# Half of the query transposes in the preceding unit, and the last output chunk in two column halves, in a pooled-attention and mixer kernel

## The chip, the cores and the metric

The kernel runs on one core of one Trainium2 chip. The metric is the device time of one execution in microseconds (us). Before the change the median of five runs is 298.71 us (297.93 to 300.1).

## What is computed

Attention over pooled keys and values, for 8 batches of 8 heads, 576 positions and head dimension 64, followed by a token MLP and a channel MLP. Inputs and output are float32.

```
pool = 8                                       # 576 keys become 72
k_p = k.reshape(B, H, 72, 8, D).mean(axis=3)
v_p = v.reshape(B, H, 72, 8, D).mean(axis=3)
attn = softmax(q @ k_p.T / sqrt(D))
x = (attn @ v_p) as (B, S, H * D)              # 576 x 512 per batch
xt = x.transpose(0, 2, 1)
h = np.maximum(xt @ w_tok1, 0) @ w_tok2        # 576 -> 256 -> 576
u = x + h.transpose(0, 2, 1)
out = u + np.maximum(u @ w_ch1, 0) @ w_ch2     # 512 -> 1536 -> 512
```

## The kernel before

**Tiling.** The 576 positions of a batch are written as (p r), with 64 values of p and 9 of r. Four chunks of 128 rows take r = 0 to 7, two values of r each; the ninth is a tail of 64 rows. Two batches share a tail tile, so the four tail tiles make up one more channel-MLP job of 512 rows.

**Units.** The program is a head, which prepares batch 0, and nine units. Unit n (function `unit`) runs the channel MLP of batch n: twelve groups of four matmuls (L412), each followed by a relu into GT on ScalarE, or on VectorE for every fourth group (L417, L419); then four output chunks of twelve matmuls (L424), each followed by an addition of u on VectorE (L429) and two output transfers on SyncE's queue (L432). Unit 8 does this for the tails. `unit_steps` is a generator that yields after every second matmul, 48 times in a unit. Steps 0 to 23 belong to the first product, six steps to each output chunk after that.

**Side work.** Between those steps the attention and token MLP of batch n+1 are put in by a table written out by hand: FIRST for unit 0, LATER for all others. A table gives, for a step number, the names of pieces of work. The order in which these are issued is the order in every engine's queue; the engines wait for each other by semaphores. The pieces that matter here:

- Q0, Q1 (`qD`, L253): transposes of the q block, from batch 2 on. VectorE turns 32x32 blocks of qb into qD. Each piece has four stream transposes and serves two of the four pairs of heads.
- kpT (L209, L211): eight small transposes of the pooled keys on TensorE, then the copy kD on VectorE.
- e0, o0 to e3, o3 (`score`, L271, L277): two score matmuls each, and the exponential on ScalarE. They read kD and qD.
- av0 to av4 (L293, L305, L311): attention product, reciprocal and scaling.
- at0, at1 (L339, L330, L332): first token product with relu, on ScalarE for at0 and VectorE for at1.
- u0 to u4 (L354, L355): second token product and the addition of x. t0 to t4 (L364, L365): the transpose of u on TensorE, and its copy into uT, which the next unit's L412 reads. u4 and t4 make the shared tail and are done for odd batches only.

**Buffers and loads.** `unit(n)` first issues the loads of batch n+2 (`load`) on GpSimd's queue: keys, the q block qb (L110) and values, then `prepare` for batch n+1: a few VectorE memsets and the pooling of keys and values on GpSimd. qb and qD have two buffers each (in the pools `raw` and `att`), so the load of qb for batch n+2 waits until the transposes of batch n are done. In PSUM `ps_one` has three buffers, `ps_two` two, and `ps_tr`, which kpT and t0 to t4 share, one.

Of the kernel before, what the change touches and what calls it, by code (L numbers as in the profile page):

```python
# [8 lines left out]
FP32 = mybir.dt.float32  # L9
BF16 = mybir.dt.bfloat16  # L10
AF = mybir.ActivationFunctionType
ALU = mybir.AluOpType
# [7 lines left out]
def kernel(  # L20
# [14 lines left out]
    nc = tc.nc  # L35
    B, H, S, D = q.shape
    P = 128
    POOL = 8
    SP = S // POOL
    BP, BR = 64, S // 64  # L40
# [4 lines left out]
    HP = H // 2  # L45
    DM = H * D
    DT = moe_w_tok1.shape[1]
    DC = moe_w_ch1.shape[1]
    NM = DC // P
# [4 lines left out]
    att = ctx.enter_context(tc.tile_pool(name="att", bufs=2))  # L54
    mix = ctx.enter_context(tc.tile_pool(name="mix", bufs=2))
    gtp = ctx.enter_context(tc.tile_pool(name="gtp", bufs=1))
    outp = ctx.enter_context(tc.tile_pool(name="outp", bufs=4))
    ps_one = ctx.enter_context(tc.tile_pool(name="ps_one", bufs=3, space=bass.MemoryType.PSUM))
# [8 lines left out]
    w_ch2 = singles.tile([P, NM, DM], BF16)  # L67
# [8 lines left out]
    loaded = {}  # L76
# [57 lines left out]
    def load_ch1():  # L134
        for g in range(3):
            cols = slice(g * 512, (g + 1) * 512)
            nc.gpsimd.dma_start(out=w_ch1[:, :, cols], in_=moe_w_ch1[:, cols].rearrange("(c p) n -> p c n", p=P))

    def load_ch2():
        for g in range(3):  # L140
            nc.gpsimd.dma_start(out=w_ch2[:, 4 * g:4 * g + 4, :],
                                in_=moe_w_ch2[g * 512:(g + 1) * 512, :].rearrange("(c p) n -> p c n", p=P))
# [19 lines left out]
    def batch_steps(b):  # L162

        par, first, by_pe = b % 2, b == 0, b < BY_PE
        st = {}
# [1 line left out]
        lower = slice(par * BP, (par + 1) * BP)  # L167

        def prepare():
            kr, vr, qb = loaded.pop(b)  # L170
            kp = att.tile([SP, H, 2, D], BF16, name="kp") if by_pe else kps[par]
            vp = att.tile([SP, H, D + 1], BF16, name="vp")
            ex = att.tile([SP, H * S + BP], BF16, name="ex")
            nc.vector.memset(vp[:, :, D], float(POOL))
            nc.vector.memset(ex[:, H * S:], 0.0)
            st.update(kp=kp, vp=vp, qb=qb, ex=ex, kr=kr, vr=vr)
            if b > 1:
                for s in ("K0", "K1", "V0", "V1"):
                    name[s]()
            if by_pe:  # L180
                st["qT"] = att.tile([P, HP, 2, EV], BF16, name="qT")
            else:
                st["qD"] = att.tile([P, HP, S], BF16, name="qD")
                st["kD"] = att.tile([P, H * SP], BF16, name="kD")
            st["AT"] = att.tile([P, 2, DM], BF16, name="AT")
            st["x"] = mix.tile([P, 4, DM], BF16, name="x")
            st["u"] = mix.tile([P, 4, DM], BF16, name="u")
            st["uT"] = mix.tile([P, 4, 4 * P], BF16, name="uT")
            if par == 0:
                tails[b // 2] = mix.tile([P, DM], BF16, name="xt")  # L190
                nc.vector.memset(tails[b // 2], 0.0)
            st["xt"] = tails[b // 2]
# [11 lines left out]
        def kpT(h0, h1):  # L204
            def go():
                ps = ps_tr.tile([P, H, SP], BF16, name="pt")
                for h in range(h0, h1):
                    row = st["kp"][:, h].rearrange("j e d -> j (e d)" if by_pe else "j e l d -> j (e l d)")
                    nc.tensor.transpose(out=ps[:, h, :], in_=row, identity=ident[0:SP, 0:SP])  # L209
                if not by_pe:  # L210
                    nc.vector.tensor_copy(out=st["kD"], in_=ps.rearrange("p h j -> p (h j)"))  # L211
                    return
                for half in range(2):
                    rows = slice(half * D, (half + 1) * D)
                    copy = nc.scalar.copy if first and half == 0 else nc.vector.tensor_copy
                    copy(out=kT[rows, half, h0 * SP:h1 * SP], in_=ps[rows, h0:h1, :].rearrange("p h j -> p (h j)"))
            return go
# [28 lines left out]
                    nc.scalar.copy(out=dst, in_=ps)  # L246
            return go

        def qD(g):
            def go():  # L250
                for ph in range(2):
                    for db in range(2):
                        nc.vector.transpose(  # L253
                            out=st["qD"][db * 64:(db + 1) * 64, 2 * g:2 * g + 2, :].rearrange(
                                "m a (r j u) -> m a r j u", u=2, r=BR)[:, :, :, :, ph],
                            in_=st["qb"][ph * 64:(ph + 1) * 64, 2 * g:2 * g + 2, 0:BR * D].rearrange(
                                "m a (r d) -> m a r d", d=D)[:, :, :, db * 32:(db + 1) * 32])
            return go

        def score(hp, odd):  # L260
# [126 lines left out]
        name = {f"kpT{g}": kpT(g * HP, (g + 1) * HP) for g in range(2)}  # L387
# [3 lines left out]
            name[f"K{g}"], name[f"V{g}"] = pool("kr", g), pool("vr", g)  # L391
        for hp in range(HP):
            name[f"q{hp}"], name[f"o{hp}"], name[f"e{hp}"] = qT(hp), score(hp, 1), score(hp, 0)
        name["Q0"], name["Q1"] = qD(0), qD(1)
        for c in range(5):
            name[f"av{c}"], name[f"u{c}"], name[f"t{c}"] = av(c), u(c), uT(c)
            name[f"at_{c}"] = at_tile(c)
# [6 lines left out]
    def unit_steps(n, st):  # L404

        GT = gtp.tile([P, NM, 4 * P], BF16, name="GT")
        uT = uT_tails if n == B else st["uT"]
        u_all = u_tails if n == B else st["u"]
        for m in range(NM):
            ps = ps_one.tile([P, 512], FP32, name="p1")  # L410
            for kk in range(4):
                nc.tensor.matmul(out=ps, lhsT=w_ch1[:, kk, m * P:(m + 1) * P], rhs=uT[:, kk, :],  # L412
                                 start=(kk == 0), stop=(kk == 3))
                if kk == 1:
                    yield
            if m % 4 != 3 or n == 0:
                nc.scalar.activation(out=GT[:, m, :], in_=ps, func=AF.Relu)  # L417
            else:
                nc.vector.tensor_scalar(out=GT[:, m, :], in0=ps, scalar1=0.0, scalar2=None, op0=ALU.max)  # L419
            yield  # L420
        for c in range(4):
            ps = ps_one.tile([P, 512], FP32, name="p1")
            for m in range(NM):
                nc.tensor.matmul(out=ps, lhsT=GT[:, m, c * P:(c + 1) * P], rhs=w_ch2[:, m, :],  # L424
                                 start=(m == 0), stop=(m == NM - 1))
                if m % 2 == 1 and m < NM - 1:
                    yield
            o_sb = outp.tile([P, DM], FP32, name="o")
            nc.vector.tensor_tensor(out=o_sb, in0=ps, in1=u_all[:, c, :], op=ALU.add)  # L429
            for half in range(2):  # L430
                b, r = (2 * c + half, 8) if n == B else (n, 2 * c + half)
                nc.sync.dma_start(out=out[b].rearrange("(p r) n -> p r n", r=BR)[:, r, :],  # L432
                                  in_=o_sb[half * BP:(half + 1) * BP, :])
            yield
# [5 lines left out]
             16: "kpT1 V0", 17: "o1", 18: "e1", 19: "q2", 20: "o2 V1", 21: "e2", 22: "q3", 23: "o3", 24: "e3",  # L440
             25: "av0", 26: "av1", 27: "av2", 28: "av3", 29: "av4", 31: "at0", 32: "at1", 34: "U0", 35: "U1",
             36: "t0 U2", 38: "t1 U3", 39: "U4", 40: "t2", 42: "t3", 46: "t4"}
    LATER = {0: "Q0", 1: "kpT", 6: "Q1", 8: "e0", 10: "o0", 12: "e1", 13: "o1", 15: "e2", 17: "o2",
             18: "e3", 20: "o3", 23: "av0", 25: "av1", 27: "av2", 29: "av3", 31: "av4", 33: "at0", 34: "at1",
             37: "u0", 38: "u1", 39: "t0", 40: "u2", 41: "t1", 42: "u3", 43: "u4 t2", 45: "t3", 47: "t4"}
    warm = singles.tile([P, 512], BF16)

    def head(s):
# [13 lines left out]
    def unit(n, at):  # L462
        side = {}
        if n + 1 < B:
            load(n + 2)
            batches[n + 1][0]()
            side = batches[n + 1][1]
        for i, _ in enumerate(unit_steps(n, batches[n][2] if n < B else None)):
            for s in at.get(i, "").split() if side else []:
                if (n + 1) % 2 or s not in ("u4", "t4"):  # L470
                    (batches[0][1][s] if n == 0 and s[0] == "u" else side[s.lower() if s[0] == "U" else s])()

    with tc.manual_schedule(engines={PE, POOLE, DVE, ACT}):
        batches = [batch_steps(b) for b in range(B)]
        nc.vector.memset(warm, 0.0)
        load(0)
        nc.vector.memset(kTs[0][D:P, 0, :], 0.0)
        nc.vector.memset(kTs[0][0:D, 1, :], 0.0)
        nc.vector.memset(w_tok1[:, 4:6, :], 0.0)
        nc.vector.memset(w_tok2t, 0.0)  # L480
        load_tok()
        load_ch1()
        permute_tok2()
        load(1)
        load_ch2()
        batches[0][0]()
        for s in HEAD.split():
            head(s)
        nc.vector.memset(kTs[1][D:P, 0, :], 0.0)
        nc.vector.memset(kTs[1][0:D, 1, :], 0.0)  # L490
        for kp in kps:
            nc.vector.memset(kp, 0.0)
        unit(0, FIRST)
        for n in range(1, B + 1):
            unit(n, LATER)


# [28 lines left out]
```

The softmax here doesn't subtract the row's maximum and nothing guards it: scores larger than these inputs give would overflow.

## Time and profile before

| | |
|---|---|
| median of five runs | 298.71 us |
| the profiled execution | 298.45 us |
| its span, first to last instruction | 296.6 us |
| TensorE busy in the span | 280.7 us |
| VectorE, ScalarE, GpSimd busy | 178.1, 97.6, 133.8 us |
| units 1 to 6, each | 29.85 to 30.7 us |
| units 7 and 8, without side work | 20.7 us and, with the end, 25.5 us |
| granted TensorE clock | 1.0 throughout |

Busy TensorE time is the sum of its recorded matmuls, whose ends are modelled, so a short loss of pace inside it doesn't show as idle. Units 2, 4 and 6 begin at 98.6, 159.4 and 220.3 us of the span, units 3 and 5 at 129.3 and 190.1 us; units 3 and 5 follow on a unit that also holds u4 and t4. Times of single instructions are given in us from the start of the span.

### The profile page before, as it was taken

To read this page: it belongs to the slowest core of one execution; us is meant where nothing else is said; L and a number is where in the kernel's file an instruction comes from. 1 tells how busy PE (TensorE), PEld (TensorE's weight loads), DVE (VectorE), ACT (ScalarE), POOL (GpSimd) and SP (SyncE) were. 2 spreads that over 40 slices of the span, in tenths; PEclk is the share of its full clock that TensorE was granted. 3 is DMA by queue.
4 is the path that set the end of the run, shared out by engine and by line. 5 is a ranking of instruction groups with operands and counts; after the bars stand their busy time and mean duration, and the time that the engine had idled before them with its cause. 6 is when DMAs were issued, how large, how long until landed. Compare 5 with 4: busy or idle time off the path is not lost.

```text
span 296.6 us, 4482 instructions
## 1 busy us (share of the span) xinstructions
PE 280.7 (95%) x1796; PEld 145.2 (49%) x1796; DVE 178.1 (60%) x332; ACT 97.6 (33%) x176; POOL 133.8 (45%) x136
## 2 busy tenths in 40 slices
PE   8789888999999999999999999999999999999993
PEld 3464354454555455445544554445455545444441
DVE  4237956678477847786758675785578556121221
ACT  2353467003900390028102810173017300502400
POOL 8285115991699069904992599993000000000000
PEclk9999999999999999999999999999999999999999
DMA  7999999947661856183827481300320021114023
GB/s 139 208 204 204 205 200 189 169 104 138 98 113 41 147 87 110 43 144 44 140 50 125 72 140 46 71 2 0 70 69 5 2 63 46 35 35 106 0 56 88
DMA packets 26868, 28.25 MB, mean 95 GB/s; under 512 B 4960, under 2 KB 21728, under 8 KB 26848
## 3 DMA queue, kind: packets, MB, share of 16 engines
q0 software_dynamic: 20512, 17.35, 40.0%
q1 hardware_dynamic: 6048, 10.03, 13.9%
q10 hardware_dynamic: 288, 0.59, 0.7%
q8 instruction: 14, 0.23, 0.3%
q14 instruction: 6, 0.05, 0.0%
HBM read 35.85 MB, written 9.44 MB: 153 GB/s over the span
## 4 chain that ended last, share of the span: by engine, by line
PE 79%; DVE 12%; ACT 4%; DMA 3%; issue 2%; POOLq 0%
PE p L424 30%; PE p L412 23%; PE p L354 6%; DVE qD L253 6%; PE p L271 5%; PE p L339 5%; PE p L293 3%; DMA kr<-in_k_dram 3%; PE pt L364 2%; DVE o L429 2%; ACT ex L277 2%; ACT GT L417 1%; DVE x L311 1%; PE pt L452 1%; DVE kD L211 1%
## 5 line engine op out<-in xcount | busy, mean ns | idle before, releaser
L424 PE MATMUL p<-w_ch,GT 128*128 128x512 bf16 x432 | 111.0, 379 | 0.0
L412 PE MATMUL p<-uT,w_ch 128*128 128x512 bf16 x384 | 95.7, 379 | 1.6 <-ACT GT L417 1.6
L417 ACT ACTIVATE GT<-p 128x512 bf16<-128x512 f32 x84 | 49.9, 594 | 106.0 <-PE p L412 93.9
L412 PEld LDWEIGHTS <-w_ch 128*128 128x128 bf16 x432 | 41.5, 98 | 38.9 <-issue 2.5
L424 PEld LDWEIGHTS <-GT 128*128 128x128 bf16 x432 | 38.7, 98 | 36.6 <-issue 0.7
L277 ACT ACTIVATE ex<-p 72x576 bf16<-72x576 f32 (+1 forms) x64 | 40.3, 645 | 14.9 <-PE p L271 13.9
L419 DVE TENSOR_SCALAR GT<-p 128x512 bf16<-128x512 f32 x24 | 16.6, 692 | 40.4 <-PE p L412 40.2
L253 DVE STREAM_TRANSPOSE qD<-qb 64x576 bf16<-64x576 bf16 x48 | 39.1, 814 | 0.7
L110 POOL DMA_DIRECT2D qb<-in_q_dram x12 | 7.6, 634 | 52.8 <-DVE qD L253 38.0
L149 POOL TENSOR_TENSOR t<-t 72x512 f32<-72x512 f32 x24 | 30.3, 1264 | 1.9
L429 DVE TENSOR_TENSOR o<-p,u 128x512 f32<-128x512 f32 x32 | 22.0, 688 | 10.3 <-PE p L424 10.2
L355 DVE TENSOR_TENSOR u<-p,x 128x512 bf16<-128x512 f32 x32 | 21.9, 688 | 6.8 <-PE p L354 6.8
L148 POOL TENSOR_TENSOR t<-kr 72x1024 f32<-72x1024 bf16 x12 | 25.5, 2126 | 0.1
L148 POOL TENSOR_TENSOR t<-vr 72x1024 f32<-72x1024 bf16 x12 | 25.4, 2118 | 0.0
L271 PE MATMUL p<-qD,kD 128*72 128x288 bf16 x96 | 19.8, 288 | 2.9 <-DVE kD L211 2.9
L311 DVE TENSOR_TENSOR x<-p,den 128x512 bf16<-128x512 f32 x30 | 20.8, 692 | 1.0
L330 ACT ACTIVATE AT<-p 128x512 bf16<-128x512 f32 x8 | 4.8, 597 | 49.7 <-PE p L339 47.0
L293 PEld LDWEIGHTS <-ex 72*128 72x128 bf16 x320 | 15.2, 98 | 10.6 <-DVE x L311 2.2
L354 PE MATMUL p<-AT,w_tok 128*128 128x512 bf16 x64 | 19.0, 379 | 0.3 <-ACT GT L417 0.3
L271 PEld LDWEIGHTS <-kD 128*72 128x72 bf16 x96 | 10.4, 113 | 15.1 <-DVE kD L211 5.8
L293 PE MATMUL p<-vp,ex 72*128 72x65 bf16 x320 | 16.9, 194 | 0.5 <-DVE x L311 0.3
L332 DVE TENSOR_SCALAR AT<-p 128x512 bf16<-128x512 f32 x8 | 5.5, 692 | 17.3 <-PE p L339 16.4
(90 smaller groups left out, 243.5 us busy)
## 6 DMA issues: line engine op xcount, KB each, us to landing
out_dram<-o SPq DMA_DIRECT2D x72, 128.0 KB, 2.4
kr<-in_k_dram POOLq DMA_DIRECT2D x7, 576.0 KB, 8.1
vr<-in_v_dram POOLq DMA_DIRECT2D x7, 576.0 KB, 9.4
qb<-in_q_dram POOLq DMA_DIRECT2D x12, 288.0 KB, 5.3
w_ch<-in_moe_w_ch_dram POOLq DMA_DIRECT2D x6, 512.0 KB, 13.4
qf<-in_q_dram SPq DMA_DIRECT2D x2, 288.0 KB, 3.1
kr<-in_k_dram POOLq DMA_DIRECT2D x2, 288.0 KB, 8.9
vr<-in_v_dram POOLq DMA_DIRECT2D x2, 288.0 KB, 11.4
```

What stands on the lines that cost most here:

```text
L148: eng.tensor_tensor(out=t4[:, 0:n], in0=t[:, hs, 0:4], in1=t[:, hs, 4:8], op=ALU.add)
L149: eng.tensor_tensor(out=t4[:, 0:n, 0:2], in0=t4[:, 0:n, 0:2], in1=t4[:, 0:n, 2:4], op=ALU.add)
L253: nc.vector.transpose(out=st["qD"][db * 64:(db + 1) * 64, 2 * g:2 * g + 2, :].rearrange("m a (r j u) -> m a r j u", u=2, r=BR)[:, :, :, :, ...
L271: nc.tensor.matmul(out=ps[0:SP, hl, 0:n], lhsT=lhsT, rhs=rhs, start=True, stop=True)
L277: nc.scalar.activation(out=dst, in_=src, func=AF.Exp, scale=scale)
L293: nc.tensor.matmul(out=halves[h // 4][:, (h % 4) * (D + 1):(h % 4 + 1) * (D + 1)], lhsT=st["ex"][:, h * S + n0:h * S + n0 + P], rhs=st["vp ...
L311: nc.vector.tensor_tensor(out=dst.rearrange("p (a h d) -> p a h d", a=2, d=D), in0=view[:, :, :, 0:D], in1=den[rows, :, :, None].broadcast ...
L354: nc.tensor.matmul(out=ps, lhsT=w, rhs=a, start=(i == 0), stop=(i == len(mms) - 1))
L412: nc.tensor.matmul(out=ps, lhsT=w_ch1[:, kk, m * P:(m + 1) * P], rhs=uT[:, kk, :], start=(kk == 0), stop=(kk == 3))
L417: nc.scalar.activation(out=GT[:, m, :], in_=ps, func=AF.Relu)
L424: nc.tensor.matmul(out=ps, lhsT=GT[:, m, c * P:(c + 1) * P], rhs=w_ch2[:, m, :], start=(m == 0), stop=(m == NM - 1))
L429: nc.vector.tensor_tensor(out=o_sb, in0=ps, in1=u_all[:, c, :], op=ALU.add)
```

## The change

There are two parts.

First, the four-instruction pieces Q0 and Q1 become eight pieces Q0 to Q7 of one stream transpose each. In unit n the first four of batch n+2 are issued as P0 to P3, at steps 33, 34, 44 and 46; the remaining Q4 to Q7 of batch n+1 stand at steps 0 and 2. The scores begin at step 5 and follow at every second step. The tile qD is taken when its first transpose is issued. Unit 1 has a table of its own, SECOND, since nobody has done the first half for batch 2: all eight transposes are in it, and the first score is at step 8. Batches 3 to 7 have their first half done by units 1 to 5.

Second, in unit 8 the last output chunk is computed in two halves of 256 columns, each with its own PSUM tile, twelve matmuls, addition and two transfers, one on SyncE's queue and one on ScalarE's.

```diff
@@ batch_steps, prepare
-            kr, vr, qb = loaded.pop(b)
+            kr, vr, qb = loaded[b]
...
-                st["qD"] = att.tile([P, HP, S], BF16, name="qD")
                 st["kD"] = att.tile([P, H * SP], BF16, name="kD")
@@ batch_steps
-        def qD(g):
-            def go():
-                for ph in range(2):
-                    for db in range(2):
-                        nc.vector.transpose(
-                            out=st["qD"][db * 64:(db + 1) * 64, 2 * g:2 * g + 2, :].rearrange(
-                                "m a (r j u) -> m a r j u", u=2, r=BR)[:, :, :, :, ph],
-                            in_=st["qb"][ph * 64:(ph + 1) * 64, 2 * g:2 * g + 2, 0:BR * D].rearrange(
-                                "m a (r d) -> m a r d", d=D)[:, :, :, db * 32:(db + 1) * 32])
+        def qD(g, ph, db):
+            def go():
+                if "qD" not in st:
+                    st["qD"], st["qraw"] = att.tile([P, HP, S], BF16, name="qD"), loaded[b][2]
+                nc.vector.transpose(
+                    out=st["qD"][db * 64:(db + 1) * 64, 2 * g:2 * g + 2, :].rearrange(
+                        "m a (r j u) -> m a r j u", u=2, r=BR)[:, :, :, :, ph],
+                    in_=st["qraw"][ph * 64:(ph + 1) * 64, 2 * g:2 * g + 2, 0:BR * D].rearrange(
+                        "m a (r d) -> m a r d", d=D)[:, :, :, db * 32:(db + 1) * 32])
             return go
...
-        name["Q0"], name["Q1"] = qD(0), qD(1)
+        for i in range(8):
+            name[f"Q{i}"] = qD(i // 4, i // 2 % 2, i % 2)
@@ unit_steps
         for c in range(4):
+            if n == B and c == 3:
+                for a in range(2):
+                    cols = slice(a * 256, (a + 1) * 256)
+                    ps = ps_one.tile([P, 512], FP32, name="p1")
+                    for m in range(NM):
+                        nc.tensor.matmul(out=ps[:, 0:256], lhsT=GT[:, m, c * P:(c + 1) * P], rhs=w_ch2[:, m, cols],
+                                         start=(m == 0), stop=(m == NM - 1))
+                    o_sb = outp.tile([P, DM], FP32, name="o")[:, 0:256]
+                    nc.vector.tensor_tensor(out=o_sb, in0=ps[:, 0:256], in1=u_all[:, c, cols], op=ALU.add)
+                    for half in range(2):
+                        (nc.scalar if half else nc.sync).dma_start(
+                            out=out[2 * c + half].rearrange("(p r) n -> p r n", r=BR)[:, 8, cols],
+                            in_=o_sb[half * BP:(half + 1) * BP, :])
+                continue
@@ tables
-    LATER = {0: "Q0", 1: "kpT", 6: "Q1", 8: "e0", 10: "o0", 12: "e1", 13: "o1", 15: "e2", 17: "o2",
-             18: "e3", 20: "o3", 23: "av0", 25: "av1", 27: "av2", 29: "av3", 31: "av4", 33: "at0", 34: "at1",
-             37: "u0", 38: "u1", 39: "t0", 40: "u2", 41: "t1", 42: "u3", 43: "u4 t2", 45: "t3", 47: "t4"}
+    LATER = {0: "Q4 Q5", 1: "kpT", 2: "Q6 Q7", 5: "e0", 7: "o0", 9: "e1", 11: "o1", 13: "e2", 15: "o2",
+             17: "e3", 19: "o3", 23: "av0", 25: "av1", 27: "av2", 29: "av3", 31: "av4", 33: "at0 P0", 34: "P1 at1",
+             37: "u0", 38: "u1", 39: "t0", 40: "u2", 41: "t1", 42: "u3", 43: "u4 t2", 44: "P2", 45: "t3", 46: "P3",
+             47: "t4"}
+    SECOND = {**LATER, 0: "Q0 Q1 Q2 Q3", 3: "Q4 Q5", 4: "Q6 Q7", 5: "", 8: "e0", 9: "o0", 10: "e1", 12: "o1", 14: "e2", 16: "o2",
+              18: "e3", 20: "o3", 7: "", 11: "", 13: "", 15: "", 17: "", 19: ""}
@@ unit
             for s in at.get(i, "").split() if side else []:
+                if s[0] == "P":
+                    if n + 2 < B:
+                        batches[n + 2][1]["Q" + s[1]]()
+                    continue
@@ main
-            unit(n, LATER)
+            unit(n, LATER if n > 1 else SECOND)
```

SECOND doesn't replace the entry 2 of LATER, so the pieces Q6 and Q7 stand at step 2 of unit 1 and again at step 4.

## The prediction

> **What bounds the kernel now.** I read the page's busy shares first, then TensorE's waits, then the chain of waits and VectorE's timeline around a unit's start, then the end of the chain.
>
> ```profile
> PE 280.7 (95%) x1796; PEld 145.2 (49%) x1796; DVE 178.1 (60%) x332; ACT 97.6 (33%) x176; POOL 133.8 (45%) x136
> ...
> PE p L271 <- DVE kD L211: 2.9, 6, 0.6
> ...
> L253 DVE STREAM_TRANSPOSE qD<-qb 64x576 bf16<-64x576 bf16 x48 | 39.1, 814 | 0.7
> ```
>
> TensorE is busy 280.7 of 296.6 us, so almost only its idle time can be won. From unit 1 to unit 6 one wait is left on it: six times 0.4 to 0.6 us, the first score (L271) waits for kD, the VectorE copy of the transposed keys (L211). kD stands behind the batch's first four stream transposes. The chain of waits shows it at the start of unit 2 (start, length, what):
>
> ```profile
> 97.91 0.69 DVE o L429
> 98.66 0.71 issue
> 99.37 0.82 DVE qD L253
> 100.20 0.82 DVE qD L253
> 101.03 0.82 DVE qD L253
> 101.89 0.47 DVE kD L211
> ```
>
> Eviction of the last output chunk, four transposes, kD: 4.4 us without a gap, while TensorE arrives at the score 0.4 us sooner. The "issue" is the first transpose, which starts under the eviction's end. Just before this VectorE has gaps (its timeline, the gap in brackets):
>
> ```profile
> 95.96 0.42 DVE L365 COPY uT<-pt 128x512 bf16<-128x512 bf16 x1
> 97.04 0.42 DVE L365 COPY uT<-pt 128x512 bf16<-128x512 bf16 x1 [0.66 <-PE pt L364]
> 97.91 0.69 DVE L429 TENSOR_TENSOR o<-p,u 128x512 f32<-128x512 f32 x1 [0.44 <-PE p L424]
> ```
>
> The end (chain, then SyncE's own queue):
>
> ```profile
> 281.50 10.37 PE p L424 x48
> 291.87 0.02 issue
> 291.90 0.69 DVE o L429
> 293.13 0.60 SPq L432 DMA_DIRECT2D out_dram<-o  x1
> ```
>
> After TensorE's last matmul come a 0.69 us eviction, two output transfers issued one after the other by SyncE, and their landing; the span ends at 296.6, 4.7 us after TensorE.
>
> **What the Trainium skill says.** "PSUM — Partial Sum Buffer", section "Engine vs sequencer instructions": VectorE's queue is strict first in, first out. The trace agrees: kD's input is on TensorE by 98.9, and the copy starts at 101.89. So what counts is where the transposes stand in VectorE's order, not when their data is there. "Perfetto Trace Analysis", section "DVE / Act Engine Instruction": a recorded span ends with the acknowledgement of the write, and the next instruction may begin before that. It agrees: a copy at 129.17 starts 0.08 us before the eviction (128.56 + 0.69) ends. Hence a transpose behind another operation adds 0.68 to 0.75 us, one behind a transpose 0.82. "DMA: Bandwidth & Descriptors", section "Issuing engines are not separate DMA queues": a second issuing engine saves only the sequencer's time; here that is the 0.5 us between two output issues.
>
> **The change part by part.**
>
> *Transposes.* Form and duration stay (814 ns). For batches 3 to 7 two of the first four (P0, P1) go to steps 33 and 34 of the preceding unit, two (P2, P3) to steps 44 and 46; the second four are split 2 + 2 over steps 0 and 2. Scores start at step 5, not 8. Batch 2 (unit 1) keeps its four transposes at step 0 and its first score at step 8, so that wait (0.63 us) stays.
>
> *Two transposes too many in unit 1.* SECOND is LATER with keys replaced, and key 2 is not among them: Q6 and Q7 stand at step 2 and again at step 4, 50 transposes in all. After kD VectorE has six instead of four. Before, it begins them at 72.78 and four take 3.32 us. Now e2, which reads what Q4 to Q7 write, must wait for the last of the six: 72.78 + 6 x 0.83 = 77.76, score at 77.80. TensorE would come to it, from the first score at 72.80, after four scores of 0.24 and six steps of 0.432: 72.80 + 0.96 + 2.59 = 76.35. So it waits 1.45 us, a wait that wasn't there. Before, e2 (one step later in the order) began at 76.83; 77.80 + 0.43 - 76.83 = +1.4 us. VectorE's relus of groups 3 and 7 come after it (from 76.13 to about 77.8), while other PSUM tiles are free: nothing more. Bounds: 0, if TensorE were late by itself, which the row of scores excludes for the most part, and 2 x 0.83 + 0.43 = 2.1.
>
> P0, P1: in unit 1 VectorE ends the last attention product at 87.19 and idles 2.49 us until at1's relu at 89.68. 0.75 + 0.82 fits. Cost nothing; if that cover were gone, u0 would wait for the relu.
>
> P2, P3 with an even batch being prepared (starts of units 2, 4, 6; no tail step). t2's copy ends at 96.38. P2 +0.75 = 97.13; t3's copy, 0.03 behind a transpose, ends at 97.58. The next unit's first matmul needs it, at 97.71: just in time. P3 to 98.33; the eviction, now 98.36 instead of 97.91, ends at 99.05. Then Q4 +0.77 (with two small memsets), Q5 +0.83, kD +0.03 +0.47 = 101.15, TensorE 0.04 later at 101.19, before 102.40. But TensorE is then at step 5: six matmuls of 0.216 (10.36 us / 48), 1.30 us of work, are still to come that before stood ahead of the score. 101.19 + 1.30 = 102.49: a loss of 0.09 us per start. TensorE arrives sooner by more than kD does. The wait is not removed, only met earlier.
>
> With an odd batch (starts of units 3 and 5) u4 and t4 are added. t2's copy ends at 127.22; P2 127.97, t3 128.42 (before 128.12), P3 129.17, eviction 129.89 (before 129.25), t4's copy +0.33 = 130.22, memsets +0.33, Q4 +0.68, Q5 +0.83, kD to 132.56, score 132.60. Plus 1.30 is 133.90 against 133.63: a loss of 0.27. There is also a wait in another place: all the small transposes share one PSUM tile (ps_tr has one buffer), so kpT stands behind t4's copy: 130.27 instead of 129.64. It lies inside the same delay and is not added.
>
> Sum: 3 x 0.09 + 2 x 0.27 = +0.8 us. Bounds for one start: nothing of the wait remains (true loss before, from the matmul pitch: 102.40 - 98.83 - 14 x 0.216 = 0.54 at even ones; 0.55 + about 0.35 hidden in modelled ends at odd ones), or the gaps of 0.66 and 0.44 us absorb nothing of P2 and P3; then kD is as late as before and the whole 1.30 is lost. I take the sums above, since each gap ended on TensorE work that doesn't move.
>
> *ScalarE in the denser scores.* A score at every second step gives one relu and one exponential in 4 x 0.216 + 0.24 = 1.10 us of TensorE, which ScalarE keeps up with now (exponentials at 102.88 and 103.98, one relu between them), at steps 8, 10, 12. Over the whole row of eight VectorE takes every fourth relu, and three PSUM tiles stand between TensorE and a late relu. Cost 0.
>
> *Loads.* qb is freed at step 2 rather than 6, so POOL, which waited 38.0 us on it in four waits, loads and pools some 3 us sooner. It isn't late now (no TensorE wait on keys or values in these units). The q block of batch n+2, which the change needs at step 33 of unit n, is issued in unit n-1 (105.99, in unit 2, for batch 5) and lands 5.5 us later. Gain 0.
>
> *The end.* Twelve matmuls of 512 columns become 24 of 256, same columns; 256-column matmuls on the same engine (L224, 8 in 0.87) run at 0.108 apart, half of 0.216: 0. The first half's eviction and transfers go under the second half's matmuls (1.3 us). Eviction after the last matmul: 0.42 (128x256, the 424 ns of L300) for 0.69: -0.27. Two issues side by side: -0.5. The last bytes 128 instead of 256 KB: the engines were busy 1.4 us for them, now 0.7, partly the same saving. In sum, SyncE's first last-chunk issue at 292.6 had the data moved by 295.1; now issue 292.35 + 1.05 to start + 0.7 = 294.1. I take -0.9. Bounds: 0 (ScalarE's queue answers slower; the trace has none of its output issues) to -1.2.
>
> **Sum.** +1.4 in unit 1, +0.8 at five starts, -0.9 at the end: +1.3. The profiled execution took 298.45 us, so 299.75; the median of the runs, 298.71, lies 0.26 above it, which gives 300.0.
>
> **Rivals.**
>
> *A, the waits are gone.* VectorE reaches kD before TensorE reaches step 5. For it: kD stands behind two transposes, not four. Against: the 1.30 us that TensorE skips. Gain 3 x 0.54 + 2 x 0.90 = 3.4, the end 0.9, unit 1 -1.4: 298.71 - 2.9 = 295.8.
>
> *B, the other side, clearly slower: VectorE late at the unit's start.* One mechanism: P2 and P3 stand ahead of t3's copy, the last eviction and t4's copy, which TensorE needs for the first L412, for kpT and for a PSUM tile; where half of the gaps is lost to them, a start costs about 0.65. 5 x 0.65 + 1.4 - 0.9 = +3.75: 302.5. With unit 1's 0.5 net it makes the kernel measurably slower from 0.2 us a start, only a little over the 0.16 that I take on average. For it: t3's copy has only 0.1 us to spare. Against: at even starts VectorE's gaps amount to 1.1 us for 1.5 us of work.
>
> *C, the end gains nothing* because landing, not issue, sets it: 298.71 + 2.2 = 300.9. For it: 2.4 us from issue to landing. Against: the engines move data for 1.4 of them.
>
> *D, the doubled transposes are hidden*, if e2 comes late anyway: 298.71 - 0.1 = 298.6. Against: TensorE has no idle time in this stretch now.
>
> **How the numbers follow.** Forecast 0.46, A 0.12, B 0.20, C 0.11, D 0.11. About 0.5% (1.5 us: 297.2 to 300.2) is what a measurement can tell from no change. The forecast alone runs from 299.0 to 301.0 (a start 0.2 us dearer or cheaper); a third of it, 0.15, lies over 300.2. Faster: the strong part of A, 0.10. Slower: B, 0.15 of the forecast and most of C, 0.44. Within: the rest of the forecast, D and what is left of A and C, 0.46. The range 297.0 to 302.2 holds the forecast, C, D and the weaker halves of A and B.
>
> **What would show it.** Right: 50 transposes; in unit 1 a wait of L271 of about 1.4 us on qD; at the later starts a VectorE stretch t2 copy, transpose, t3 copy, transpose, eviction without gaps, and TensorE still waiting 0.4 us and more for kD; kpT waiting on t4's copy at units 3 and 5; at1's relu no later; some 3.8 us from TensorE's end to the span's end. Wrong: no waits of L271 on kD after unit 1 (A); a wait of L412 on uT's copy, or units longer by over 0.5 us (B); still 4.7 us at the end (C); no wait on qD (D).

## The result and the profile after

The changed kernel takes 299.55 us (median of 44 runs, 298.17 to 303.34); the kernel before, measured beside it, 298.12 us. The ratio is 1.0051, with a 95% interval of 1.0038 to 1.0065; it leaves out runs more than 1.5% above the fastest of their kernel. That is slower by 1.5 us: the interval excludes no change, but the size lies at the edge of the 0.5% that the prediction took as what a measurement can tell.

The two spans, 296.6 and 298.9 us, can't be subtracted as they stand. The head, which is the same code in both, differs from one execution to the next: the first matmul of unit 0 comes at 29.63 us in the profile before and at 30.56 in the one after. So I count from that matmul on: 267.02 us to the end before, 268.36 after, +1.34 us.

Three answers of the trace after correspond to those shown above. First the page's busy times and the group of the transposes:

```profile
PE 282.0 (94%) x1808; PEld 146.9 (49%) x1808; DVE 178.7 (60%) x335; ACT 99.6 (33%) x176; POOL 133.6 (45%) x136
...
L252 DVE STREAM_TRANSPOSE qD<-qb 64x576 bf16<-64x576 bf16 x50 | 40.6, 812 | 0.9
```

There are 50 transposes, two more than before. TensorE's waits after (us in total, times, longest):

```profile
PE p L270 <- DVE kD L210: 2.5, 6, 0.6
...
PE pt L208 <- DVE uT_tails L364: 1.3, 2, 0.7
...
PE p L270 <- DVE qD L252: 1.1, 1, 1.1
```

The wait for kD is still there six times, 2.5 us instead of 2.9: 0.63 us in unit 1 as before, 0.49 us at units 2, 4 and 6 (before 0.38), and only 0.17 to 0.18 us at units 3 and 5 (before 0.55 to 0.56). Two waits are new: kpT (L208) for t4's copy, 0.66 us each at units 3 and 5, and a single one of a score for qD. VectorE's and TensorE's lines of the timeline after show this last wait, in unit 1. First VectorE:

```profile
73.21 0.46 DVE L210 COPY kD<-pt 128x576 bf16<-128x576 bf16 x1
73.58 5.04 DVE L252 STREAM_TRANSPOSE qD<-qb 64x576 bf16<-64x576 bf16 x6
78.65 0.69 DVE L419 TENSOR_SCALAR GT<-p 128x512 bf16<-128x512 f32 x1
```

Then TensorE, after the same moment:

```profile
76.21 0.41 PE L270 MATMUL p<-qD,kD 128*72 128x288 bf16 x2
76.46 1.07 PE L412 MATMUL p<-uT,w_ch 128*128 128x512 bf16 x4
78.67 0.44 PE L270 MATMUL p<-qD,kD 128*72 128x288 bf16 x2 [1.15 <-DVE qD L252]
```

Six transposes run without a gap behind kD. The fifth pair of scores, e2, starts 0.05 us after the last of them, and TensorE stands idle before it.

The start of unit 2, VectorE's and TensorE's lines of the timeline after; the next unit's first L412 is at 100.01:

```profile
98.26 0.42 DVE L364 COPY uT<-pt 128x512 bf16<-128x512 bf16 x1
98.72 0.82 DVE L252 STREAM_TRANSPOSE qD<-qb 64x576 bf16<-64x576 bf16 x1
...
99.45 0.38 DVE L364 COPY uT<-pt 128x512 bf16<-128x512 bf16 x1
99.86 0.82 DVE L252 STREAM_TRANSPOSE qD<-qb 64x576 bf16<-64x576 bf16 x1
...
100.70 0.69 DVE L443 TENSOR_TENSOR o<-p,u 128x512 f32<-128x512 f32 x1
...
103.00 0.46 DVE L210 COPY kD<-pt 128x576 bf16<-128x576 bf16 x1
...
103.52 0.44 PE L270 MATMUL p<-qD,kD 128*72 128x288 bf16 x2 [0.49 <-DVE kD L210]
```

Both bracketed gaps of before are filled. The eviction (L443) starts 0.69 us after the unit's first matmul instead of 0.20. kD comes sooner than before, but TensorE is there sooner too, and waits.

The end, VectorE and the queues in the timeline after:

```profile
293.86 0.42 DVE L430 TENSOR_TENSOR o<-p,u_tails 128x256 f32<-128x256 f32 x1 [0.62 <-PE p L427]
294.32 1.81 ACTq L432 DMA_DIRECT2D out_dram<-o  x2
294.47 1.61 SPq L432 DMA_DIRECT2D out_dram<-o  x2
295.17 0.42 DVE L430 TENSOR_TENSOR o<-p,u_tails 128x256 f32<-128x256 f32 x1 [0.89 <-PE p L427]
```

The last eviction starts 3.75 us before the end of the span (298.92 - 295.17); before it was 4.75 (296.65 - 291.90).

The time by units. A unit is counted from its first L412 to the next unit's first L412 (the marks of units 2 to 6 given ahead of the prediction lie 0.7 to 0.9 us later, so their lengths differ a little from these), the end from the start of the last eviction, the sum from the first L412 of unit 0 to the end of the span. The kernels e1 to e8 are those of the experiments below.

| us | unit 1 | unit 2 | unit 3 | unit 4 | unit 5 | unit 6 | end | sum |
|---|---|---|---|---|---|---|---|---|
| before | 29.85 | 30.88 | 29.95 | 30.88 | 29.96 | 30.88 | 4.75 | 267.02 |
| after | 31.23 | 31.03 | 30.20 | 31.04 | 30.22 | 30.99 | 3.75 | 268.36 |
| e1 | 29.89 | 31.05 | 30.21 | 31.06 | 30.22 | 30.99 | | 267.07 |
| e2 | 29.85 | 30.88 | 29.95 | 30.89 | 29.95 | 30.89 | | 266.03 |
| e3 | 29.85 | 30.36 | 29.84 | 30.36 | 29.84 | 30.31 | | 264.18 |
| e4 | 29.88 | 30.50 | 29.58 | 30.51 | 29.59 | 30.50 | | 264.20 |
| e5 | 29.89 | 30.31 | 29.21 | 30.31 | 29.21 | 30.31 | | 262.87 |
| e6 | 29.24 | 30.31 | 29.21 | 30.31 | 29.21 | 30.31 | | 262.23 |
| e7 | 29.84 | 30.88 | 29.94 | 30.88 | 29.96 | 30.87 | 4.26 | 266.53 |
| e8 | 29.85 | 30.87 | 29.94 | 30.88 | 29.96 | 30.88 | 4.59 | 266.84 |

Unit 0 takes 38.2 us and unit 7 20.72 us in all of them. The end takes 3.74 to 3.76 us in e1 to e6. After against before: unit 1 +1.38, units 2 to 6 together +0.93, the end -1.00.

### The profile page after: what moved, and what is told of

Its sections match the earlier page's. It is cut to its first block, busy times and chain, and to the rows that moved or that the text cites. A ratio compares the mean times of both kernels' runs of the same rounds, so it can differ in the third digit from the quotient of the medians.

```text
span 298.9 us, 4516 instructions
## 1 busy us (share of the span) xinstructions
PE 282.0 (94%) x1808; PEld 146.9 (49%) x1808; DVE 178.7 (60%) x335; ACT 99.6 (33%) x176; POOL 133.6 (45%) x136
## 4 chain that ended last, share of the span: by engine, by line
PE 74%; DVE 16%; ACT 4%; issue 3%; DMA 2%; POOLq 0%
PE p L438 25%; PE p L412 24%; DVE qD L252 7%; PE p L353 5%; PE p L270 5%; PE p L338 5%; PE p L292 3%; DVE o L443 2%; DMA kr<-in_k_dram 2%; ACT ex L276 2%; DVE uT L364 2%; PE pt L469 1%; ACT GT L417 1%; PE pt L363 1%; DVE x L310 1%
## 5 line engine op out<-in xcount | busy, mean ns | idle before, releaser
L438 PE MATMUL p<-w_ch,GT 128*128 128x512 bf16 x420 | 108.4, 379 | 0.0
L412 PE MATMUL p<-uT,w_ch 128*128 128x512 bf16 x384 | 95.8, 379 | 1.6 <-ACT GT L417 1.6
L412 PEld LDWEIGHTS <-w_ch 128*128 128x128 bf16 x432 | 41.4, 98 | 39.0 <-issue 2.6
L438 PEld LDWEIGHTS <-GT 128*128 128x128 bf16 x420 | 37.5, 98 | 35.1 <-issue 0.7
L252 DVE STREAM_TRANSPOSE qD<-qb 64x576 bf16<-64x576 bf16 x50 | 40.6, 812 | 0.9
L443 DVE TENSOR_TENSOR o<-p,u 128x512 f32<-128x512 f32 x32 | 22.0, 688 | 8.2 <-PE p L438 8.0
L469 PE MATMUL pt<-warm 128*128 128x512 bf16 x36 | 12.5, 467 | 3.0 <-DVE kTs L215 1.8
```

What stands on the lines that cost most here:

```text
L252: nc.vector.transpose(out=st["qD"][db * 64:(db + 1) * 64, 2 * g:2 * g + 2, :].rearrange("m a (r j u) -> m a r j u", u=2, r=BR)[:, :, :, :, ...
```

## The experiments

The theory has three parts: unit 1 waits for the doubled transposes (M); at the other starts the wait for kD remains, since the scores were moved ahead by more than kD, and P2 and P3 hold up VectorE just there (K); the end gains by the smaller last piece and the second queue. Each has a rival in the expectation.

### e1: the doubled transposes issued once

```diff
-    SECOND = {**LATER, 0: "Q0 Q1 Q2 Q3", 3: "Q4 Q5", 4: "Q6 Q7", ...
+    SECOND = {**LATER, 0: "Q0 Q1 Q2 Q3", 2: "", 3: "Q4 Q5", 4: "Q6 Q7", ...
```

> The change with one edit: entry 2 of SECOND is emptied, so Q6 and Q7 of batch 2 are issued once. Theory M (e2 waits for the doubled transposes): unit 1 takes 29.9 us again instead of 31.2, no wait of the scores on qD is left, 48 transposes, and the time falls by 1.4 us against the change: ratio to the kernel before 1.000 (0.999 to 1.002). Rival R (unit 1 lost its time because e0, o0 and e1 stand in three steps running): unit 1 stays at 31.2 us, the ratio at 1.005.

Measured: unit 1 29.89 us, 48 transposes, no wait of the scores on qD, and the sum 1.29 us below that of the change. The ratio to the kernel before is 1.0019 (0.9988 to 1.0049). The scores e0, o0 and e1 stand in three steps running here too, so rival R falls. These two instructions cost as much as the whole change lost against the kernel before; without them it is level with it, not faster, since the loss at the other starts (+0.93) and the gain at the end (-1.00) about cancel.

### e2: the end alone

The kernel before, with the block for `n == B and c == 3` of the change and nothing else.

> The kernel before with nothing but the two column halves and two queues of the last chunk. Theory (smaller last eviction, issues side by side): 4.1 us from the last matmul of GT to the end of the span instead of 5.2, ratio 0.9965. Rival C (landing sets the end): 5.2 us and ratio 1.000.

Measured: 4.05 us from the start of the last matmul to the end of the span (before 5.17), the units as before to 0.01 us, the sum 0.99 us less. The ratio is 0.9974 (0.9946 to 1.0003), in which such a difference is just not resolved; the trace has it. Rival C falls.

### e3: the scores back at their old steps

```diff
-    LATER = {0: "Q4 Q5", 1: "kpT", 2: "Q6 Q7", 5: "e0", 7: "o0", 9: "e1", 11: "o1", 13: "e2", 15: "o2",
-             17: "e3", 19: "o3", 23: "av0", ...
+    LATER = {0: "Q4 Q5", 1: "kpT", 2: "Q6 Q7", 8: "e0", 10: "o0", 12: "e1", 13: "o1", 15: "e2", 17: "o2",
+             18: "e3", 20: "o3", 23: "av0", ...
-    SECOND = {...}
+    SECOND = {**LATER, 0: "Q0 Q1 Q2 Q3", 2: "", 6: "Q4 Q5 Q6 Q7"}
```

> The change with Q6 and Q7 once, and the scores back at their steps of before (8, 10, 12, 13, 15, 17, 18, 20), P0 to P3 as in the change. Theory K (the wait for kD stayed since the first score was moved six matmuls ahead): at units 2, 4 and 6 the wait for kD is gone, 4.15 to 4.2 us from the unit's first matmul to its first score instead of 4.70; at units 3 and 5 kpT still waits 0.6 us for t4's copy, and the score comes at 4.9 to 5.05 us instead of 5.05. About -1.6 us in the units, -1.1 at the end: ratio 0.991. Rival L (P2 and P3 hold up the unit's beginning wherever the scores stand): units as long as in the change, ratio 1.000.

Measured: 0.9906 (0.9879 to 0.9933). From the unit's first matmul to its first score it takes 4.15 us at units 2, 4 and 6 and 4.96 at units 3 and 5. TensorE's waits of e3:

```profile
PE pt L468 <- DVE kTs L215: 1.7, 2, 0.8
PE p L412 <- ACT GT L417: 1.6, 3, 0.7
PE p L223 <- DMA kr<-in_k_dram: 1.4, 1, 1.4
PE pt L208 <- DVE uT_tails L364: 1.3, 2, 0.7
PE p L270 <- ACT qT L245: 1.2, 2, 0.8
PE pt L468 <- DVE warm L495: 1.2, 1, 1.2
PE p L270 <- DVE kD L210: 0.6, 1, 0.6
```

Of the six waits for kD only that of unit 1 is left; kpT's two waits for t4's copy stay at 1.3 us. With the transposes of batches 3 to 7 where they are in e1, and the scores later by up to three steps, the sum is 2.9 us less (267.07 to 264.18). The first score accounts for nearly all of it: with the 1.30 us of six matmuls that come after it there, it stood at 3.51 + 1.30 = 4.81 us in e1's unit 2, 0.66 later than here, and that unit is 0.69 us longer. So at units 2, 4 and 6 what kept the wait was not that transposes were moved but that the scores were moved with them. Rival L falls for units 2, 4 and 6; at 3 and 5, where P3 stands ahead of t4's copy, e3 wins only 0.1 us over the kernel before, so there it holds in part.

### e4: the four transposes in VectorE's idle stretches

```diff
-             17: "e3", 19: "o3", 23: "av0", ... 33: "at0 P0", 34: "P1 at1", ... 44: "P2", 45: "t3", 46: "P3",
+             17: "e3", 18: "P0", 19: "o3", 20: "P1", 23: "av0", ... 33: "at0 P2", 34: "P3 at1", ... 45: "t3",
-    SECOND = {...}
+    SECOND = {... 2: "", ... 18: "e3 P0", 20: "o3 P1", ...}
```

> The change with Q6 and Q7 once, and P0 to P3 at steps 18, 20, 33 and 34, in VectorE's two idle stretches of 3.7 and 2.5 us, none at 44 and 46. Theory K and its second half (P2 and P3 push t3's copy, the last eviction and t4's copy): first score 3.05 us after the unit's start at units 2, 4, 6 (change: 3.50), 3.6 at units 3 and 5 (change: 4.0), kpT no longer waits for t4's copy; about -1.7 us against before in the units, -1.1 at the end: ratio 0.9905. Rival (where the four transposes stand ahead of the unit makes no difference): 3.5 and 4.0 us as in the change, ratio 1.000.

Measured: first score at 3.02 us (units 2, 4, 6) and 3.37 to 3.39 (3 and 5), the latter better than expected; ratio 0.9917 (0.9891 to 0.9942), sum 2.8 us below the kernel before. The start of unit 3 in e4, VectorE's and TensorE's lines of its timeline:

```profile
131.11 0.41 DVE L364 COPY uT_tails<-pt 128x512 bf16<-128x512 bf16 x1
...
131.58 0.42 PE L208 MATMUL pt<-ident,kps 72*128 72x72 bf16 x8
...
133.90 0.44 PE L270 MATMUL p<-qD,kD 128*72 128x288 bf16 x2 [0.17 <-DVE kD L210]
```

The copy and kpT in the change, where unit 3 starts at 131.05:

```profile
132.26 0.42 DVE L364 COPY uT_tails<-pt 128x512 bf16<-128x512 bf16 x1
...
132.73 0.42 PE L208 MATMUL pt<-ident,kps 72*128 72x72 bf16 x8 [0.66 <-DVE uT_tails L364]
```

There the copy ran 1.21 us after the unit's first matmul, and kpT waited for it; in e4 it is at 0.58 us (131.11 - 130.53), and kpT shows no wait. So the place of P2 and P3 is the other half of K. e3 and e4 reach the same sum by different ways: in one TensorE comes to the score later, in the other VectorE comes to kD sooner.

### e5 and e6: nothing ahead of kD

e4 left room in VectorE's idle stretches. e5 puts six transposes there, so that none stands ahead of kD:

```diff
+    LATER = {1: "kpT", 2: "Q6 Q7", 5: "e0", ... 15: "o2", 16: "P0", 17: "e3 P1", 18: "P2", 19: "o3 P3",
+             23: "av0", ... 33: "at0 P4", 34: "P5 at1", ...}
```

SECOND has its eight transposes once, and P0 to P3 at steps 16 to 19.

> Six of the eight transposes in the preceding unit, all in VectorE's idle stretches (four at steps 16 to 19, two at 33 and 34), only Q6 and Q7 left at step 2, none ahead of kD; scores from step 5. Theory K: kD is ready before TensorE comes to the first score, 2.85 us after the unit's start at units 2, 4 and 6 and about 3.1 at units 3 and 5, no wait for kD there; about 1 us less than with two transposes ahead of kD, 3.8 us less than before from the first unit's start to the end: ratio 0.987. Rival (the idle stretches are too short, and the relu of group 11 or the attention products are held up): units 30 us and more, ratio 0.992 or above.

Measured: 0.9869 (0.9816 to 0.9922), first score at 2.85 and 3.04 us, and the wait for kD left in unit 1 alone. The start of unit 2 in e5, from its timeline:

```profile
102.81 0.46 DVE L210 COPY kD<-pt 128x576 bf16<-128x576 bf16 x1 [0.37 <-PE pt L208]
103.30 1.66 DVE L252 STREAM_TRANSPOSE qD<-qb 64x576 bf16<-64x576 bf16 x2
...
104.33 0.41 PE L270 MATMUL p<-qD,kD 128*72 128x288 bf16 x2
```

Now VectorE waits for TensorE (0.37 us), and kD is done 1.06 us ahead of the score. The four transposes in the idle stretch don't hold up the relu of group 11, for which VectorE still waits on TensorE (unit 1):

```profile
81.77 3.31 DVE L252 STREAM_TRANSPOSE qD<-qb 64x576 bf16<-64x576 bf16 x4
85.23 0.69 DVE L419 TENSOR_SCALAR GT<-p 128x512 bf16<-128x512 f32 x1 [0.15 <-PE p L412]
```

The rival falls.

e6 adds batch 2: two of its transposes in unit 0 (`31: "at0 P0", 32: "P1 at1"`), two ahead of kD in unit 1, first score at step 6.

> The same, and two of batch 2's transposes in unit 0 (steps 31 and 32), so that unit 1 has two ahead of kD and its first score at step 6. If the block of batch 2 has landed by then: unit 1 0.5 to 0.7 us shorter than 29.85, ratio 0.985. If it has not, unit 0 grows beyond 38.2 us by the lateness.

Measured: unit 1 29.24 us, 0.65 less than in e5, unit 0 unchanged at 38.2. The sum is 4.79 us below the kernel before, the smallest of all. The ratio, 0.9874 (0.9816 to 0.9933), can't set it apart from e5.

### e7 and e8: the two halves of the end

e7 is e2 with all four transfers on `nc.sync`. e8 is the kernel before with one edit:

```diff
-                nc.sync.dma_start(out=out[b]...
+                (nc.scalar if n == B and c == 3 and half else nc.sync).dma_start(out=out[b]...
```

> The kernel before with the last chunk in two column halves, all transfers on SyncE's queue. If the smaller eviction and the smaller transfers save 0.6 of the 1.1 us and the second queue 0.5: 4.6 us from the last matmul of GT to the end of the span (before 5.2, both parts 4.05). If the queue is all: 5.1.

> The kernel before with the last chunk whole, its two transfers on two queues. If the second queue saves the 0.5 us between the issues: 4.7 us from the last matmul of GT to the end. If landing of the data sets the end: 5.1.

Measured, from the start of the last matmul as in e2: 4.57 us for e7, as expected; 5.0 for e8, which is nearly what the rival said. These two kernels were run once each. In e8 both issues stand side by side, at the end of its timeline:

```profile
292.22 0.47 SPq L432 DMA_DIRECT2D out_dram<-o  x1
292.23 0.54 ACTq L432 DMA_DIRECT2D out_dram<-o  x1
```

The end of each kernel, from the start of the last eviction, divided at the issue and the landing of the transfer that lands last:

| us | eviction to issue | issue to landing | landing to end | together |
|---|---|---|---|---|
| before | 1.23 | 2.36 | 1.16 | 4.75 |
| halves, one queue (e7) | 1.17 | 2.04 | 1.04 | 4.26 |
| whole, two queues (e8) | 0.72 | 2.64 | 1.23 | 4.59 |
| halves, two queues (after) | 0.46 | 2.19 | 1.11 | 3.75 |

The halves alone save 0.5 us, the second queue alone 0.16, both together 1.0. In e8 the last issue comes 0.5 us sooner, but its transfer takes 0.28 us longer to land. The packets of ScalarE's queue begin only at 293.95, when those of SyncE's, which begin at 293.35, are nearly through (294.17). With the halves the second queue is worth 0.5 us (4.26 to 3.75), for two reasons. The landing is lengthened by 0.15 us only. And the issue gains 0.71 us instead of 0.5: in e7 SyncE also issues the first half's two transfers, and the last two stand behind them. So this comparison isn't one of transfer size alone.

## Why the prediction was right

It said 300.0 us and a change of +1.3; the runs gave a ratio that makes it +1.5, the traces +1.34. Step by step:

- **Two transposes too many in unit 1**, +1.4: unit 1 is 1.38 us longer, and e1 takes this away with those two alone. The score was put 5.00 us after the first one; it came at 4.95 (78.67 - 73.72). TensorE's wait was put at 1.45 us; 1.15 are recorded, 1.35 counted by the 0.216 us from matmul to matmul, since the recorded end of the last one is modelled.
- **P0 and P1**, nothing: right. at1's relu still waits for TensorE, 0.92 us where it was 2.49.
- **The wait is not removed, only met earlier**, +0.09 at the starts of units 2, 4 and 6: first score 3.50 us after the unit's first matmul, plus the 1.30 of six matmuls, 4.80 against 4.70. Right, and e3 shows the cause. The sign named for it, a wait for kD of 0.4 us and more, is there at these three starts (0.49) but not at units 3 and 5 (0.17 to 0.18), where kpT's wait takes its place.
- **P3 ahead of t4's copy**, +0.27 at units 3 and 5: 4.00 + 1.30 against 5.05, +0.25. The wait of kpT was put at 130.27 - 129.64 = 0.63 us; it is 0.66.
- **The sum of the five starts**, +0.8: units 2 to 6 are 0.93 longer. Units 2 and 4 lose some 0.05 more at their own ends, where t4's transposes wait for t3's later copy. The working has this copy 0.30 us later but charges nothing for it.
- **The end**, -0.9: -1.00. The terms fit too: the last issue comes 0.77 us sooner, as 0.27 for the eviction and 0.5 for the queue had it, and the smaller transfer adds 0.23. But they belong together: e8 shows that the second queue without the halves gives 0.16 us, e7 that the halves without it bring the last issue only 0.06 us forward.
- **Loads**, nothing: right. In unit 2 the q block is asked for 5.4 us after the unit's first matmul instead of 8.3, and TensorE's waits on loads don't change.

That the sum fits to 0.1 us is in part luck: the five starts cost 0.13 us more than put, and the end gained 0.1 more.

Of the rivals, A (the waits are gone) and C (no gain at the end) didn't happen, nor did D (the doubled transposes hidden). B's mechanism is there at units 3 and 5, at well under half of the price it was given (0.25 for 0.65). That the kernel as a whole came out on the slow edge of what can be measured was in the sum, which left 0.44 for slower; the most likely verdict, within 0.5%, stands at its edge with a ratio of 1.0051.

The time that the waits for kD held was there to be won, though not by these steps: with the transposes where VectorE idles, and none in front of kD, e5 and e6 are 1.3% faster than the kernel before (six runs each; both intervals reach from 0.982 to 0.992 or 0.993). The prediction priced this as rival A, 3.4 us at the five starts; in e5 units 2 to 6 are 3.2 us shorter.

## What to carry to other kernels

When a producer and its consumer are both moved ahead, compare the two shifts: a wait shrinks only by as much as the producer gains more than the consumer. Move work off a critical stretch into a gap that the timeline shows, not into the stretch just ahead of it on the same queue: two gaps of 0.66 and 0.44 us ahead of work that the next unit needs are not a place for two instructions of 0.82 us; at the start of unit 2 they brought the last eviction 0.49 us later. And where a table is made from another by replacing entries, count the instructions in the profile: two more transposes than before cost more than the rest of the change won.

## What the runs showed of the hardware

- Savings at the end of this kernel are not additive: 0.49 us for the halves, 0.16 us for the second queue, 1.00 us for both. Two transfers of 128 KB issued side by side on two queues (e8) landed 2.31 and 2.64 us after their issue, and the packets of the second began when those of the first were nearly through.
- The head, the same code in all kernels, took 28.9 to 33.4 us to unit 0's first matmul in these ten profiles, and the longer heads went with a lower mean clock granted over the span: 28.86 us at 1.000 (e2), 30.56 at 0.994 (after), 31.92 at 0.988 (e4), 33.37 at 0.981 (e5). The low clock lies in the head: between 10 and 20 us of the span it is 1.00, 0.83, 0.66 and 0.59 in these four, and 1.00 in all of them from 29 us on. Units 2 to 6 repeat to 0.02 us where the code around them is the same. Effects of a few tenths of a us are seen in unit lengths long before they are seen in run times. What sets the clock and the head's length wasn't tried.
